# Attention in 64x64 quarters of the array: 21 blocks of 64 keys of four heads a batch instead of 24 blocks of 112 keys of two heads

## The chip, the cores and the metric

The kernel runs on one core of a Trainium2 chip. The time is device microseconds (us) of one execution. Three runs of the kernel before gave 609.70, 611.04 and 614.22 us: a median of 611.04. TensorE (PE in the profile, its weight loads PEld) multiplies matrices out of SBUF into the eight PSUM banks, ScalarE (ACT) and VectorE (DVE) read those banks, GpSimd (POOL) and SyncE (SP) mainly start DMA transfers; POOL also does some arithmetic on SBUF.

## The reference

`q`, `k` and `v` are float32 [8 batches, 12 heads, 448 tokens, 64]. Per batch and head the reference computes

```
scores = (q @ k.T) / 8
attn   = max(scores, 0)**2 / 448          # no softmax, so blocks of keys simply add up
x[b, :, head*64:(head+1)*64] = attn @ v
```

and then, per batch, on x [448, 768]:

```
u   = x + real(fft(fft(x, over tokens), over channels))
un  = (u - mean(u)) / sqrt(var(u) + 1e-6)             # per token
out = u + max(un @ w_ch1, 0) @ w_ch2                  # 768 -> 3072 -> 768
```

All 8 x 448 tokens go through the two large products (the FFN below).

## The kernel before

**Order of the work.** The kernel is one long unrolled program. Its order is found while it is built by a planner, `Streams.run` (lines 79 to 111). Each stage is a generator that yields `need(engine, duration, deps, buffers, ok)`. The planner keeps a time for each engine, takes the stage that could start earliest (ties by a rank), moves that engine's time by the duration and lets the generator issue its instructions. So the durations written in the code (`mm`, `act`, `dve`, `SWITCH = 0.13`, 0.85 for a load) only decide the order; the chip runs each engine's instructions in that order and waits where data are late. The stages are `loading` (POOL), `turning` (transposes of q and k), `attention(b)`, `mix(b)` with `mix_rows` (both transforms, the sum u, its normalisation), `ffns`, and `warming`, which puts idle matmuls (line 1135) wherever PE has nothing else before the first batch is through. `attention(b)` may run ahead of the FFN by up to `LEAD = 1.9` batches: `progress` counts finished FFN work in batches.

**PSUM.** `BS` is three pairs of banks (tiles `psS`, [128, 2, 512]) and `BF` two single banks (tiles `psF`). Scores, the transforms and `mix_rows` use BS; the FFN, the values and the transposes of q and k on PE use BF.

**Loads** (`load_group`, line 303). A batch has three groups of four heads. For each group and each of q, k, v there is one DMA from POOL, which also turns float32 into bf16. The tile has R = 112 partitions with 4 heads x 4 neighbouring tokens x 64 numbers: runs of 1 KB read, 512 bytes written.

**Turning q and k.** For batches 0 and 1 on PE (`turn_on_pe`, line 424: 16 transposes of 112x64 for each half of a group, both q and k in one BF bank, then one copy to SBUF, line 429, on DVE or ACT). For later batches DVE reorders the tile (`qkr`, line 392) and SP starts a DMA transpose into `qkT` (line 401).

**Attention** (`attention`, from line 485). A *block* is 112 keys (every fourth token) of a pair of heads against all 448 queries; a batch has `NB = 4 * MC` = 24.
- Scores, line 540: two matmuls of 64 contraction rows by 112 columns, one head in each half of the array's rows, 448 queries streamed, into the two banks of a BS pair.
- `squares`: ACT takes the relu of both heads from PSUM (line 561, 112 x 896), DVE squares it (line 567). `NSQ` = 9 such tiles.
- Values, line 525: for one pair of heads, four blocks, each two matmuls of 112 contraction rows by 64 columns, one head in each half of the array's columns, added up in one BF bank.
- `fold` (lines 448 to 471): DVE takes that bank out with two scaled copies (`xT`, tokens back in order, the second half reversed), adds and subtracts the two halves (lines 459, 460), and in the second half of a batch combines the two of them (`diff`, lines 469, 471). `turn_x` (line 480) starts a DMA transpose of `xT` from SP.

One step of `attention` is a *burst* on PE: if four squared blocks wait, their values, then up to three blocks of scores, then back to the FFN. For batch 0 (`few`) scores come singly and before values. When six values are done, `mix(b)` follows: line 954 (line 929 for batch 0), 970, then `mix_rows` 794 to 846, stores to DRAM and DMA transposes back (`turn_un`, line 892), and `ffn(b)` with its products in lines 1085 and 1113.

**SP and POOL** take their DMA issues in the planner's order, each waiting for its data at the head of its queue.

Of the kernel before, what the change touches and what calls it, by code (L numbers as in the profile page):

```python
# [10 lines left out]
BF16 = mybir.dt.bfloat16  # L11
# [126 lines left out]
def kernel(  # L138
# [20 lines left out]
    HG = 4  # L159
    NG = H // HG  # L160
# [123 lines left out]
    GRP = 4 * R * HG * Dh * 4  # L284
# [4 lines left out]
    def load_group(i, which=(0, 1, 2)):  # L289

        b, g = divmod(i, NG)
        hs = slice(g * HG, (g + 1) * HG)
        for x, (nm, src) in enumerate((("q", q), ("k", k), ("v", v))):
            if x not in which:
                continue
            if b == 0 and x < 2:
                e = yield need("POOL", 0.85)
                t = first_qk[x][:R, g]
            else:
                e = yield need("POOL", 0.85, bufs=[BQ[x]])  # L300
                t = work.tile([R, HG, 4 * Dh], BF16, name=f"{nm}n", tag=f"{nm}n",
                              bufs=3 if nm == "v" else QN)
            nc.gpsimd.dma_start(out=t, in_=src[b, hs].rearrange("h (p j) d -> p h (j d)", j=4))  # L303
            loads[i][x] = t.rearrange("p h (j d) -> p j h d", j=4)

            ready[i][x].t = sch.dma(e, GRP, 360e3, "sw") + (1.5 if g else 0.0, 3.0, 14.0, 7.0)[min(b, 3)]
            if i == 0 and x == 1:
                yield need("POOL", 0.7)
                make_identity(nc, ident)
            if i == 0 and x == 2:  # L310
                e = yield need("POOL", 1.1)
                dft_indices()
                indices_ready.t = e + LATENCY["POOL"]
            if i == 2 and x == 2:
                yield need("POOL", 0.75)
                pads()
            if i == NG + 1 and x == 1:
                yield need("POOL", 1.8)
                mirrors()


    first_qk = [work.tile([128, NG, HG, 4 * Dh], BF16, name="qk0", tag="unT", bufs=2) for _ in range(2)]
# [42 lines left out]
    NSQ = 9  # L365
# [14 lines left out]
    def turning():  # L380

        for b in range(B):
            for g in range(NG):
# [5 lines left out]
                for x in range(2):  # L389
                    e = yield need("DVE", 0.42, [ready[b * NG + g][x]], [BQR] if x == 0 else [])  # L390
                    o = work.tile([R, 4, HG, Dh], BF16, name="qkr", tag=f"qkr{x}", bufs=QR)
                    nc.vector.tensor_copy(o, loads[b * NG + g][x])
                    BQ[x].free.append(e)
                    qk.append(o.rearrange("p c h d -> p (c h d)"))
                ts = []
                for x in range(2):
                    e = yield need("SP", 0.8, [e + LATENCY["DVE"]], [BQT] if x == 0 else [])
                    if x == 0:
                        both = work.tile([128, 2, 8, R], BF16, name="qkT", tag="qkT", bufs=2)
                    t = both[:, x]  # L400
                    nc.sync.dma_start_transpose(out=t, in_=qk[x])
                    ts.append(t.rearrange("q (c r) p -> q r c p", r=2))
                    e = sch.dma(e + 0.5, R * 2048, 180e3)
# [5 lines left out]
    def turn_on_pe(b, g):  # L409
# [3 lines left out]
        both = work.tile([128, 2, 8, R], BF16, name="qkT", tag="qkT", bufs=2)  # L413
        turned[b][g] = [both[:, x].rearrange("q (c r) p -> q r c p", r=2) for x in range(2)]
        for r in range(2):
            for x in range(2):
                e1 = yield need("PE", 4 * 0.07, ready[i][x:x + 1], [] if x else [BF],
                                lambda: b != 1 or tail[0] == 2 or tail[0] == 0 and g == 0)
                if x == 0:
                    ptf = BF.take()  # L420
                    pt = ptf.bitcast(BF16)
                for c in range(4):
                    for h in range(2):
                        nc.tensor.transpose(pt[h * Dh:(h + 1) * Dh, x * S + c * R:x * S + (c + 1) * R],  # L424
                                            loads[i][x][:, c, 2 * r + h, :], ident[:R, :R])

            en, copy = (("DVE", nc.vector.tensor_copy), ("ACT", nc.scalar.copy))[r if b > 0 or g == 0 else 0]
            e2 = yield need(en, 0.75 if en == "DVE" else act(2 * S), [e1 + LATENCY["PE"]])
            copy(both.rearrange("q x (c r) p -> q r x c p", r=2)[:, r],
                 pt[:, 0:2 * S].rearrange("q (x c p) -> q x c p", x=2, c=4))  # L430
            BF.give(ptf, e2)
            turned_at[b][g][r].t = e2 + LATENCY["ACT"]
# [9 lines left out]
    def fold(b, m, F, av, av_end):  # L442
        e1 = yield need("DVE", 2 * dve(HS) + 2 * dve2(NS), [av_end],
                        [BX[m]] + ([BA[m]] if m < 3 else []))
        x = xTc[m]

        at = av[:, 0:S].rearrange("q (j p) -> q p j", j=4)
        nc.vector.tensor_scalar(x[:, 0:HS].rearrange("q (p j) -> q p j", j=4), at[:, 0:R // 2],  # L448
                                1.0 / (64.0 * S), None, op0=ALU.mult)
        xb, ab = x[:, XH + 1:XH + NS].rearrange("q (p j) -> q p j", j=4), at[:, R - 1:R // 2 - 1:-1, ::-1]  # L450
        nc.vector.tensor_scalar(xb, ab, 1.0 / (64.0 * S), None, op0=ALU.mult)  # L451
        BF.give(av, e1 - 2 * dve2(NS))
        if b > 0:
            sch.add(turn_x(b, m, e1 - 2 * dve2(NS) + LATENCY["DVE"]), (1, 1))
        else:
            x_ready[b][m].t = e1 + LATENCY["DVE"]
# [28 lines left out]
    def attention(b):  # L485


        F, sqs, fresh = [], {}, []
        NB = 4 * MC
        p = pa = 0  # L490
        while pa < NB:
            few = b == 0 or progress[0] == 0.0
            n = min(1 if few else 3, NB - p)
            ma = pa // 4

            lag = 3 if few else 2 if b < 3 else 1
            old = fresh[-lag] if len(fresh) >= lag else 0
            values = pa + 4 <= old if n else True
            n = max(0, min(n, NSQ - (p - pa - 4 * values)))
            values = values or not n  # L500
            fresh.append(p + n)
            deps, bufs, dur = [], [], 0.0
            if values:
                deps += [sqs[i][1] for i in range(pa, pa + 4)]
                bufs.append(BF)
                if b == 1:
                    deps.append(first_mixed)
                deps.append(ready[b * NG + ma // 2][2])
                dur += 4 * mm(S) + SWITCH
            if n:  # L510
                deps += [turned_at[b][i // 8][i // 4 % 2] for i in (p, p + n - 1)]
                bufs += [BS] * n
                dur += n * mm(S) + SWITCH
            lead = b + (p if n else pa) / NB - LEAD
            e = yield need("PE", dur + SWITCH, deps, bufs, lambda: progress[0] >= lead and (b != 1 or tail[0] == 2))
            av_end, scs = None, []

            for part in ("scores", "values") if few else ("values", "scores"):
                if part == "values" and values:
                    av = BF.take()  # L520
                    vn, h0 = loads[b * NG + ma // 2][2], 2 * ma % HG
                    for c in range(4):
                        sq = sqs.pop(pa + c)[0]
                        for h in range(2):
                            nc.tensor.matmul(av[h * Dh:(h + 1) * Dh, 0:S], lhsT=vn[:, c, h0 + h, :],  # L525
                                             rhs=sq[:, h, :], start=(c == 0), stop=(c == 3))
                        BSQ.free.append(e)
                    av_end = e - (n * mm(S) + SWITCH if n and not few else 0.0) + LATENCY["PE"]
                    if ma % 2 == 1:
                        BQ[2].free.append(e)  # L530
                    pa += 4
                if part == "values":
                    continue
                for i in range(p, p + n):
                    m, c = divmod(i, 4)
                    qT, kT = turned[b][m // 2]
                    sc = BS.take()
                    for h in range(2):
                        ps = slice(h * Dh, (h + 1) * Dh)
                        nc.tensor.matmul(sc[:R, h, 0:S].rearrange("k (c q) -> k c q", c=4),  # L540
                                         lhsT=kT[ps, m % 2, c, :], rhs=qT[ps, m % 2],
                                         start=True, stop=True)
                    scs.append((i, sc, e - SWITCH - (4 * mm(S) + SWITCH if values and few else 0.0)
                                - (p + n - 1 - i) * mm(S)))
                    if c == 3 and m % 2 == 1:
                        BQT.free.append(e)
                    if b == 0 and i == NB - 1:
                        first_scores.t = e
# [5 lines left out]
            if av_end is not None:  # L554
                yield from fold(b, ma, F, av, av_end)

    def squares(scs, sqs):
        for i, sc, t in scs:
            e = yield need("ACT", act(2 * S) - 0.03, [t + LATENCY["PE"]], [BSQ])
            r = sqs[i][0] = work.tile([R, 2, S], BF16, name="sq", tag="sq", bufs=NSQ)  # L560
            nc.scalar.activation(r, sc[:R, :, 0:S], AF.Relu)  # L561
# [578 lines left out]
    with tc.manual_schedule():  # L1140
# [8 lines left out]
        sch.add(attention(0), (0, 0))  # L1149
# [35 lines left out]
```

## Time and profile before

| | |
|---|---|
| median of three runs | 611.04 us |
| the profiled execution: its own time | 611.72 us |
| its span (first to last instruction) | 609.9 us |
| granted TensorE clock, mean | 0.997 of full speed |
| PE busy / weight loads | 596.6 us (98%) / 350.6 us (57%) |
| DVE busy | 338.6 us (56%) |
| ACT busy | 295.3 us (48%) |
| POOL busy | 156.7 us (26%) |
| DMA packets | 125,283, of them 40,304 on POOL's queue |
| FFN matmuls, lines 1085 and 1113 | 231.0 and 225.4 us busy |
| scores, line 540 / values, line 525 | 384 matmuls, 52.1 us / 384 matmuls, 45.5 us busy |

Busy time of PE counts the modelled length of each matmul, which overlaps the next one: 98% says that PE is rarely without work, not that it works at its peak. What matmuls cost is read from the distance between their starts. The page also has the chain that ended last: it goes back from the last instruction to what released it, and so on to the beginning; its shares say which lines set the end.

The time falls into parts that do not have the same limit: up to 9.4 us the first loads, to 39.5 us the attention of batch 0, to 59 us its transforms, from then on the FFN with the attention of later batches between its matmuls, and after 503.5 us the FFN alone.

### The profile page before, as it was taken

To read this page: it belongs to the slowest core of one execution; us is meant where nothing else is said; L and a number is where in the kernel's file an instruction comes from. 1 tells how busy PE (TensorE), PEld (TensorE's weight loads), DVE (VectorE), ACT (ScalarE), POOL (GpSimd) and SP (SyncE) were. 2 spreads that over 40 slices of the span, in tenths; PEclk is the share of its full clock that TensorE was granted. 3 is DMA by queue.
4 is the path that set the end of the run, shared out by engine and by line. 5 is a ranking of instruction groups with operands and counts; after the bars stand their busy time and mean duration, and the time that the engine had idled before them with its cause. 6 is when DMAs were issued, how large, how long until landed. Compare 5 with 4: busy or idle time off the path is not lost.

```text
span 609.9 us, 10759 instructions
## 1 busy us (share of the span) xinstructions
PE 596.6 (98%) x4314; PEld 350.6 (57%) x4314; DVE 338.6 (56%) x766; ACT 295.3 (48%) x448; POOL 156.7 (26%) x201
## 2 busy tenths in 40 slices
PE   8998999999999899999999999999999999999997
PEld 6567766577665465555445565555445565654464
DVE  6975776945688659555734468655743447110011
ACT  5965762387534567436653247535762245014300
POOL 8433031401246118211720127110620007000000
PEclk9998999999999999999999999999999999999999
DMA  9999999727978995977584675975461215420022
GB/s 128 207 209 228 209 171 156 177 68 103 136 154 179 191 183 164 178 134 120 172 152 104 121 125 190 150 153 98 144 136 60 87 51 174 115 93 14 1 81 76
DMA packets 125283, 82.22 MB, mean 135 GB/s; under 512 B 76352, under 2 KB 113248, under 8 KB 125232
## 3 DMA queue, kind: packets, MB, share of 16 engines
q0 software_dynamic: 40304, 34.02, 35.0%
q1 hardware_dynamic: 84928, 47.50, 33.8%
q8 instruction: 34, 0.56, 0.4%
q14 instruction: 17, 0.14, 0.1%
HBM read 62.91 MB, written 26.64 MB: 147 GB/s over the span
## 4 chain that ended last, share of the span: by engine, by line
PE 82%; DMA 6%; DVE 5%; issue 2%; POOL 2%; ACT 1%; SPq 1%; DVEq 0%; POOLq 0%; ACTq 0%
PE psF L1085 34%; PE psF L1113 32%; PE psF L525 6%; PE psS L540 6%; PE psS L954 2%; DMA w<-in_moe_w_ch_dram 2%; PE psS L794 1%; DMA qn<-in_q_dram 1%; DVE stats L826 1%; DMA vn<-in_v_dram 1%; DMA unT<-nbot 1%; DMA ntop<-un 1%; DVE u L815 1%; POOL qk L303 1%; DVE sq L567 1%
## 5 line engine op out<-in xcount | busy, mean ns | idle before, releaser
L1085 PE MATMUL psF<-unT,w 128*128 128x256 bf16 (+3 forms) x1440 | 231.0, 317 | 3.2 <-DMA unT<-nbot 2.0
L1113 PE MATMUL psF<-w,hT 128*128 128x384 bf16 (+2 forms) x1344 | 225.4, 326 | 0.0
L561 ACT ACTIVATE sq<-psS 112x896 bf16<-112x896 f32 x192 | 164.8, 917 | 119.6 <-PE psS L540 119.4
L1085 PEld LDWEIGHTS <-w 128*128 128x128 bf16 x1440 | 133.3, 99 | 94.3 <-issue 16.4
L1113 PEld LDWEIGHTS <-hT 128*128 128x128 bf16 x1344 | 129.0, 98 | 93.2 <-issue 10.2
L1047 ACT ACTIVATE hT<-psF 128x512 bf16<-128x512 f32 (+1 forms) x177 | 98.0, 555 | 108.8 <-PE psF L1085 107.6
L567 DVE TENSOR_TENSOR sq<-sq 112x896 bf16<-112x896 bf16 x192 | 119.3, 639 | 44.6 <-ACT sq L561 43.4
L1056 DVE TENSOR_TENSOR o<-psF,o 128x384 f32<-128x384 f32 (+2 forms) x56 | 31.0, 554 | 108.7 <-PE psF L1113 108.0
L303 POOL DMA_DIRECT2D vn<-in_v_dram x24 | 17.3, 721 | 177.3 <-PE psF L525 159.7
L448 DVE TENSOR_SCALAR xT<-psF 128x224 bf16<-128x224 f32 x48 | 18.8, 391 | 66.6 <-PE psF L525 66.6
L540 PE MATMUL psS<-qkT 64*112 64x448 bf16 x384 | 52.1, 366 | 2.3 <-ACT unT L780 1.5
L814 POOL TENSOR_TENSOR u<-tp,xn 128x385 f32<-128x385 f32 (+1 forms) x14 | 16.3, 1167 | 116.6 <-DVE tp L805 104.8
L525 PE MATMUL psF<-sq,vn 112*64 112x448 bf16 x384 | 45.5, 359 | 0.0
L540 PEld LDWEIGHTS <-qkT 64*112 64x112 bf16 x384 | 20.5, 125 | 26.4 <-issue 20.6
L525 PEld LDWEIGHTS <-vn 112*64 112x64 bf16 x384 | 17.6, 109 | 21.3 <-issue 13.6
L843 POOL TENSOR_SCALAR un<-u,rstd,nmr 128x768 bf16<-128x768 f32 (+1 forms) x24 | 28.0, 1170 | 6.2 <-DVE nmr L835 5.9
L826 DVE BATCH_NORM_STATS2 stats<-u 128x6 f32<-128x384 f32 (+1 forms) x56 | 28.1, 538 | 0.0
L303 POOL DMA_DIRECT2D qn<-in_q_dram x21 | 15.4, 734 | 13.9 <-PE psF L424 8.6
L1135 PE MATMUL psS<-warm 128*128 128x126 bf16 (+1 forms) x206 | 17.7, 239 | 1.3 <-DVE warm L216 1.3
L451 DVE TENSOR_SCALAR xT<-psF 128x224 bf16<-128x224 f32 x48 | 18.5, 386 | 0.0
L1135 PEld LDWEIGHTS <-warm 128*128 128x128 bf16 x206 | 13.5, 108 | 6.3 <-issue 4.6
L303 POOL DMA_DIRECT2D kn<-in_k_dram x21 | 15.3, 728 | 2.6 <-DVE diff L469 1.5
(120 smaller groups left out, 366.9 us busy)
## 6 DMA issues: line engine op xcount, KB each, us to landing
out_dram<-o SPq DMA_DIRECT2D x24, 384.0 KB, 2.3
vn<-in_v_dram POOLq DMA_DIRECT2D x24, 224.0 KB, 5.1
qn<-in_q_dram POOLq DMA_DIRECT2D x21, 224.0 KB, 6.4
kn<-in_k_dram POOLq DMA_DIRECT2D x21, 224.0 KB, 7.3
w<-in_moe_w_ch_dram POOLq DMA_DIRECT2D x12, 384.0 KB, 13.7
w<-in_moe_w_ch_dram POOLq DMA_DIRECT2D x4, 1152.0 KB, 22.2
utop<-u SPq DMA_DIRECT2D x8, 384.0 KB, 2.4
o<-utop SPq DMA_DIRECT2D x7, 384.0 KB, 4.7
```

The lines of the kernel that those rows point to most:

```text
L303: nc.gpsimd.dma_start(out=t, in_=src[b, hs].rearrange("h (p j) d -> p h (j d)", j=4))
L525: nc.tensor.matmul(av[h * Dh:(h + 1) * Dh, 0:S], lhsT=vn[:, c, h0 + h, :], rhs=sq[:, h, :], start=(c == 0), stop=(c == 3))
L540: nc.tensor.matmul(sc[:R, h, 0:S].rearrange("k (c q) -> k c q", c=4), lhsT=kT[ps, m % 2, c, :], rhs=qT[ps, m % 2], start=True, stop=True)
L561: nc.scalar.activation(r, sc[:R, :, 0:S], AF.Relu)
L567: nc.vector.tensor_tensor(r, r, r, op=ALU.mult)
L826: nc.vector.bn_stats(stats[:n, hf, :], u[:n, hf * (D // 2):(hf + 1) * (D // 2)])
L843: nc.gpsimd.tensor_scalar(un[:n], u[:n], rstd[:n, i:i + 1], nmr[:n, i:i + 1], op0=ALU.mult, op1=ALU.add)
L1047: nc.scalar.activation(h, p, AF.Relu)
L1056: nc.vector.tensor_tensor(o[:, hs], pc[:, 0:w], o[:, hs], op=ALU.add)
L1085: nc.tensor.matmul(ph[:, i * w:(i + 1) * w], lhsT=w1_sb[m][hf][:, jj * 128:(jj + 1) * 128], rhs=unT[:, m, c0:c0 + w], start=(m == 0), stop ...
L1113: nc.tensor.matmul(pc[:, 0:w], lhsT=hT[j // 4][:, j % 4, c * 128:(c + 1) * 128], rhs=w2_sb[j // 6][:, j % 6, hs], start=(j == 0), stop=(j ...
L1135: nc.tensor.matmul(first_pps[0][:, t, c0:512], lhsT=warm[:, 0:128], rhs=warm[:, c0:512], start=not begun, stop=False)
```

## The change

Every group of four heads is now laid out on all 128 partitions: partition (m, p) holds head pair m of the group and seven neighbouring tokens (J = 7 = 448/64). A block becomes 64 keys of all four heads, 7 blocks a group, 21 a batch.

- Loads: two DMAs for each of q, k, v, one for the even and one for the odd heads, with runs of 7 x 64 numbers.
- Scores: four matmuls of 64 rows by 64 columns. Values: four of 64 rows by 64 columns; the two row halves write different banks, so a group's values (seven blocks, four heads) take a pair of banks. For batches from 1 on that is a BS pair instead of a BF bank; for batch 0 it is both BF banks.
- Squares: 21 tiles of 128 x 896 a batch instead of 24 of 112 x 896; NSQ is 10.
- Turning: on PE, 14 transposes of 128x64 each for q and for k, each in a BF bank with its own copy; by DMA, a 128 x 896 source instead of 112 x 1024.
- `fold` handles a group: two head pairs, their four scaled copies, then the additions (`fold_one`). Six folds a batch as before, but two of them become ready together.
- A burst has seven blocks of values and up to two of scores, or up to three of scores alone. Batch 0 has its own `first_attention` and `first_values`; in its last group the values are given in two parts, six blocks and one.

The core of the diff:

```diff
+    J = S // 64
...
-                t = work.tile([R, HG, 4 * Dh], BF16, name=f"{nm}n", tag=f"{nm}n",
+                t = work.tile([128, 2, J * Dh], BF16, name=f"{nm}n", tag=f"{nm}n",
                               bufs=3 if nm == "v" else QN)
-            nc.gpsimd.dma_start(out=t, in_=src[b, hs].rearrange("h (p j) d -> p h (j d)", j=4))
-            loads[i][x] = t.rearrange("p h (j d) -> p j h d", j=4)
+            for h in range(2):
+                if h:
+                    e = yield need("POOL", 0.72)
+                nc.gpsimd.dma_start(out=t[:, h], in_=src[b, hs].rearrange("(m h) (p j) d -> h m p (j d)", h=2, j=J)[h])
+            loads[i][x] = t.rearrange("p h (j d) -> p j h d", j=J)
...
-    NSQ = 9
+    NSQ = 10
...
-                    o = work.tile([R, 4, HG, Dh], BF16, name="qkr", tag=f"qkr{x}", bufs=QR)
+                    o = work.tile([128, J, 2, Dh], BF16, name="qkr", tag=f"qkr{x}", bufs=QR)
...
+        for x in range(2):
+            e1 = yield need("PE", 2 * J * 0.04, ready[i][x:x + 1], [BF],
+                            lambda: b != 1 or tail[0] == 2 or tail[0] == 0 and g == 0)
+            ptf = BF.take()
+            pt = ptf.bitcast(BF16)[:, 0:J * 128].rearrange("q (j p) -> q j p", j=J)
+            for j in range(J):
+                for h in range(2):
+                    nc.tensor.transpose(pt[h * Dh:(h + 1) * Dh, j, :], loads[i][x][:, j, h, :], ident)
+
+            en, copy = (("DVE", nc.vector.tensor_copy), ("ACT", nc.scalar.copy))[x if b > 0 or g == 0 else 0]
...
+    def fold(b, g, F, avs, av_end, give):
+        for h in range(2):
+            m = 2 * g + h
+            e1 = yield need("DVE", 2 * dve(HS), [av_end], [BX[m]])
...
+            give(h, e1)
+            if b > 0:
+                sch.add(turn_x(b, m, e1 + LATENCY["DVE"]), (1, 1))
+            else:
+                x_ready[b][m].t = e1 + LATENCY["DVE"]
+                yield from fold_one(b, m, F)
+        if b > 0:
+            for h in range(2):
+                yield from fold_one(b, 2 * g + h, F)
...
-        NB = 4 * MC
+        NB = NG * J
         p = pa = 0
         while pa < NB:
+            few = progress[0] == 0.0
+            g = pa // J
+            values = pa + J <= p - 2 or p == NB
+            n = min(1 if few else 2 if values else 3, NB - p, NSQ - (p - pa - J * values))
             deps, bufs, dur = [], [], 0.0
             if values:
+                deps += [sqs[i][1] for i in range(pa, pa + J)] + [ready[b * NG + g][2]]
                 if b == 1:
                     deps.append(first_mixed)
+                bufs.append(BS)
+                dur += J * mm(S) + SWITCH
             if n:
+                deps += [c for i in (p, p + n - 1) for c in turned_at[b][i // J]]
                 bufs += [BS] * n
+                dur += n * mm(S)
             lead = b + (p if n else pa) / NB - LEAD
             e = yield need("PE", dur + SWITCH, deps, bufs, lambda: progress[0] >= lead and (b != 1 or tail[0] == 2))
+            if values:
+                held = BS.take()
+                avs = [held[:, m] for m in range(2)]
+                weigh(b, g, avs, sqs, range(J))
...
+            if values:
+                yield from fold(b, g, F, avs, e - n * mm(S) + LATENCY["PE"], lambda m, t: BS.give(held, t) if m else None)
+
+    def score(b, i, e):
+        g, j = divmod(i, J)
+        qT, kT = turned[b][g]
+        sc = BS.take()
+        for h in range(2):
+            ps = slice(h * Dh, (h + 1) * Dh)
+            for m in range(2):
+                ks = slice(m * 64, (m + 1) * 64)
+                nc.tensor.matmul(sc[ks, h, 0:S].rearrange("k (j p) -> k j p", j=J),
+                                 lhsT=kT[ps, j, ks], rhs=qT[ps, :, ks], start=True, stop=True)
...
+    def weigh(b, g, avs, sqs, js):
+        vn = loads[b * NG + g][2]
+        for j in js:
+            sq = sqs[g * J + j][0]
+            for m in range(2):
+                ks = slice(m * 64, (m + 1) * 64)
+                for h in range(2):
+                    nc.tensor.matmul(avs[m][h * Dh:(h + 1) * Dh, 0:S], lhsT=vn[ks, j, h, :],
+                                     rhs=sq[ks, h, :], start=(j == 0), stop=(j == J - 1))
+
+    def first_attention():
+
+        F, sqs = [], {}
+        for i in range(NG * J):
+            e = yield need("PE", mm(S), turned_at[0][i // J], [BS])
+            sqs[i] = [None, Cell()]
+            sch.add(squares([(i, score(0, i, e), e)], sqs), (0.2, 0.2))
+            if i % J == J - 1:
+                sch.add(first_values(i // J, F, sqs), (0.1, 0.1))
+        first_scores.t = e
+
+    def first_values(g, F, sqs):
+        held = None
+        for js in ((0, J),) if g < NG - 1 else ((0, J - 1), (J - 1, J)):
+            e = yield need("PE", (js[1] - js[0]) * mm(S),
+                           [sqs[g * J + j][1] for j in range(*js)] + [ready[g][2]], [BF, BF] if js[0] == 0 else [])
+            if held is None:
+                held = [BF.take(), BF.take()]
+            weigh(0, g, held, sqs, range(*js))
+            BSQ.free += [e] * (js[1] - js[0])
+        BQ[2].free.append(e)
+        yield from fold(0, g, F, held, e + LATENCY["PE"], lambda m, t: BF.give(held[m], t))
...
-            r = sqs[i][0] = work.tile([R, 2, S], BF16, name="sq", tag="sq", bufs=NSQ)
-            nc.scalar.activation(r, sc[:R, :, 0:S], AF.Relu)
+            r = sqs[i][0] = work.tile([128, 2, S], BF16, name="sq", tag="sq", bufs=NSQ)
+            nc.scalar.activation(r, sc[:, :, 0:S], AF.Relu)
...
-        sch.add(attention(0), (0, 0))
+        sch.add(first_attention(), (0, 0))
```

## The prediction

> **What bounds the kernel now.** First the page's busy table, the chain and the groups.
>
> ```profile
> PE 596.6 (98%) x4314; PEld 350.6 (57%) x4314; DVE 338.6 (56%) x766; ACT 295.3 (48%) x448; POOL 156.7 (26%) x201
> ...
> PE 82%; DMA 6%; DVE 5%; issue 2%; POOL 2%; ACT 1%; SPq 1%; DVEq 0%; POOLq 0%; ACTq 0%
> ...
> L561 ACT ACTIVATE sq<-psS 112x896 bf16<-112x896 f32 x192 | 164.8, 917 | 119.6 <-PE psS L540 119.4
> ...
> L303 POOL DMA_DIRECT2D qn<-in_q_dram x21 | 15.4, 734 | 13.9 <-PE psF L424 8.6
> ```
>
> PE is the bound: 82% of the chain is PE work, and ACT's relu of the scores waits 119.4 us for PE, not the reverse. Then the waits of PE itself over the whole span:
>
> ```profile
> PE psF L1085 <- DMA unT<-nbot: 2.0, 1, 2.0
> PE psF L424 <- DVE qkT L429: 1.9, 1, 1.9
> PE psS L540 <- ACT unT L780: 1.5, 1, 1.5
> ```
>
> There are three real stalls, and all lie where a batch's FFN begins: at 51 us (batch 0, second part), 119 us (batch 1) and 208 us (batch 2). There a chain of DVE, ACT, SP and DMA steps is later than PE. From 210 us PE never waits again for more than 0.9 us. So a nanosecond of PE work is worth a nanosecond after 210 us, and maybe less before.
>
> Then the timeline of PE in a quiet stretch, where starts are what counts:
>
> ```profile
> 299.69 2.54 PE L1085 MATMUL psF<-unT,w 128*128 128x512 bf16 x11
> 302.16 0.95 PE L525 MATMUL psF<-sq,vn 112*64 112x448 bf16 x8
> 303.03 0.78 PE L540 MATMUL psS<-qkT 64*112 64x448 bf16 x6
> 303.74 2.55 PE L1085 MATMUL psF<-unT,w 128*128 128x512 bf16 x11
> ```
>
> Values start at 302.16, scores at 303.03, FFN at 303.74: four pairs in 0.87 us, three pairs in 0.71. Inside a burst the starts of single matmuls show the two of a pair 3 ns apart and pairs 189 ns apart: 448 columns at full rate, two matmuls at once. What is left over is the change of shape: the last pair of values is followed after 0.283 us instead of 0.189, and the first pair of scores takes 0.045 more than the others. So a stretch of scores costs 0.71 - 3 x 0.189 = 0.143 us beyond its pairs, one of values 0.87 - 0.756 = 0.12.
>
> **PE work, batches 1 to 7.** I summed the stretches of lines 525 and 540 in PE's timeline, from the first start of a stretch to the next instruction of another line:
>
> | from, us | values matmuls | scores matmuls | bursts | time, us |
> |---|---|---|---|---|
> | 59 to 119.4 | 48 | 54 | 10 | 11.4 |
> | 119.4 to 210.2 | 80 | 84 | 16 | 20.4 |
> | 210.2 to the end | 208 | 198 | 38 | 46.2 |
>
> Together 78.0 us for 336 pairs (63.5 us) and 98 stretches (14.5 us). After the change there are 7 x 42 = 294 groups of four matmuls. Going through the loop of `attention` with 21 blocks gives nine bursts a batch (three with values), as many as now, but scores and values have one shape, so a burst is one stretch: 63 x 0.143 = 9.0 us. What four matmuls on quarters cost no row shows. Lower end: 189 ns, all four at once. Upper end: 378 ns, two pairs in turn. I take 189, because both halves of it stand in the rows: scores run concurrently in two row halves, values in two column halves, each at 189 ns. Issue doesn't forbid it: the transposes of line 424 (eight q and eight k matmuls in 0.45 us from 68.63 to 69.08, each with its own weights) start every 25 ns, so four start in 100 ns. Sum: 294 x 0.189 + 9.0 = 64.6 us, against 78.0: **-13.4 us**, by the same working about -7.2 of it after 210 us and -6.2 before.
>
> **Weight loads** are four for each block instead of two, each half as wide for scores. In the values burst above the rows are:
>
> ```profile
> 302.15 0.52 PEld L525 LDWEIGHTS <-vn 112*64 112x64 bf16 x8 [0.42 <-issue]
> ```
>
> All eight loads are over by 302.67, before the last pair of matmuls starts at 302.75: they lie under matmuls in the same rows of the array. A rule of the Trainium skill speaks against the change here: "TensorE: Matmul & The Clock Gate", Part 3 (packing small matmuls), says that a weight load overlaps running matmuls only when it is for other rows of the array, and column neighbours share their rows. By that rule the present values would show it too, and this row disagrees. What the rule would give is rival 2.
>
> **Batch 0, to 39.5 us.** PE isn't the bound: line 1135's idle matmuls fill its gaps. From 9.4 to 36.0 us ACT is: its 24 relus take 20.2 us of that stretch, 0.84 each, and DVE is nearly as full. Three relus fewer: -2.5 us. Against it: the last fold covers two head pairs one after another, which puts another two copies and two additions (0.71 + 0.46 us by the spacing in rows 448 to 460) behind the last values, while the last values are one block, not four (-0.57): +0.6. The loads: 26 issues instead of 13 on POOL, whose queue also holds the identity matrix and the indices from which DVE and ACT build the transforms' tables.
>
> ```profile
> 8.64 0.70 POOL L303 DMA_DIRECT2D vn<-in_v_dram  x1
> ...
> 17.70 0.53 POOL L332 DMA_DIRECT2D w<-in_moe_w_ch_dram  x1 [0.33 <-DMA vn<-in_v_dram]
> ```
>
> A load of 448 runs costs 0.70 us to issue, a weight load of 128 rows 0.53. The new ones have 128 runs of 1.8 KB, so they are nearest to 0.53; the bounds are 0.53 and 0.70, a pair costing 0.36 to 0.70 us more than one now. Over the six loads of q and k up to the third group, and the v loads between, that is 3 to 5 us at the last issue, but today the DMA engines, not POOL, set the pace: 448 packets of 512 bytes take 1.15 us at the rate from 15 to 20 us (about 390 packets a microsecond), and for the last of these loads, issued at 8.64, POOL still waits at 17.70. The new 256 packets of 896 bytes, between 60 ns (512 bytes) and 134 ns (1,536 bytes) a packet about 88 ns, take 0.97 us. So the later issue is mostly hidden by that queue: 0 to +2.6 us, I take +1.3. Sum for batch 0: -0.6 us. If the tables come later than the relus, the 1.3 grows, and that is in the range.
>
> **From 59 to 210 us** the -6.2 us is not all kept. The stalls at 119 and 208 us end chains from the last values of a batch through fold, the transforms, normalisation and transposes. PE that is faster only waits longer there, unless the last values come earlier too. The last fold now has two head pairs: 1.4 us of copies, 0.9 of additions, 1.6 of combining, against 2.05 in the rows from 97.08 to 99.13: about +2 us on the chain to line 954. For the other side, the last values of batch 1 should come some 2 us earlier (nine bursts at today's spacing). I keep half: -3.1 us.
>
> **Nothing for:** ACT and DVE after 59 us (three relus and squares fewer a batch, but off the path: ACT is under 50% and DVE under 60% busy from 210 us); the DMA transposes of q and k (same bytes) and their DVE copies; the PE transposes of batches 0 and 1 (28 of 128 columns for 32 of 112); POOL's extra 0.36 us a load later on, since POOL idles 103.3 us for values there. Values holding a BS pair take it from scores for seven blocks (1.3 us) and the fold's copies (1.4); a burst comes every 8 us or so against ACT's 2.5 us for three blocks, so the FFN covers it. If that cover is gone, bursts come later in the FFN, and PE still has FFN work until a batch's end.
>
> **Sum** against the profiled execution's 611.72 us (span 609.9 and 1.8 around it): -7.2 - 3.1 - 0.6 = -10.9, so 600.8. That execution is 0.7 us above the median of the runs; I forecast **600.5**.
>
> **Rivals.**
> 1. *The gain of the first 210 us is lost to the chains* and the first batches are late as well: -7.2, loads +2.6, two stalls 2 us longer: about 611. For it: all three stalls are there. Against: batch 0 has less ACT work. Chance 0.15.
> 2. *The weight load of a quarter is not hidden* (slower). Each block then pays 109 ns (line 525's mean load) on top of 189: 294 x 0.298 + 9 = 96.6 us of attention, +18.6: 630 us. The gain is gone from about 234 ns a block, (78.0 - 9.0) / 294. Against it: the row of loads above; for it: nothing here shows four shapes at once. It is what the rule of the Trainium skill named above would give. Chance 0.09.
> 3. *The quarters don't run four at once*, so that the change doesn't do what it says: 378 ns a block, 120 us, +42: 653 us. Chance 0.05.
> 4. *Batch 0's new order stalls* (both BF banks held by values while the next turning wants one): 4 us of held banks (seven blocks, four copies, an addition) in each of two groups, 8 us: 609. Chance 0.05.
>
> The forecast's own case, 593 to 606, has 0.66. The range 592 to 616 takes in rivals 1 and 4 and leaves out 2 and 3. A measurement of this kernel tells about 1% (6 us) from no change. Faster by over 1% (under 605): 0.65, the forecast's case without its last microsecond; within: 0.21, that and rivals 1 and 4; slower: 0.14, rivals 2 and 3.
>
> **What would show it.** Four matmuls of 64*64 some 3 ns apart and the next four 189 ns later; no 0.28 us between values and scores; nine bursts a batch, one of values each seven blocks. ACT's last relu of batch 0 at about 34 us instead of 36.0. Line 1085 first at 45 to 47 us. PE's stall at batch 2 two or three us longer. After 210 us the FFN reaching its end about 7 us sooner. The prediction is wrong if blocks start over 200 ns apart, or if a new stall of several microseconds stands before 120 us.

## The result, and the profile after

The changed kernel takes **738.62 us** (median of four runs, 736.77 to 743.42), the kernel before 611.63 (four runs beside it): a ratio of 1.2085, with an interval from 1.2009 to 1.2161. It is 21% slower where 2% faster was forecast, outside the range (592 to 616) and slower than any rival (653 at most). The profiled execution took 743.42 us, its span 741.6.

The lines of its page that answer to those shown before. In the new code scores are line 542, values 555, the relu 585, the FFN 1109 and 1137, the loads 307:

```profile
PE 623.0 (84%) x4988; PEld 366.2 (49%) x4988; DVE 330.5 (45%) x742; ACT 276.7 (37%) x424; POOL 214.7 (29%) x273
...
DMA packets 241640, 82.82 MB, mean 112 GB/s; under 512 B 206528, under 2 KB 229600, under 8 KB 241584
...
q0 software_dynamic: 156656, 34.54, 52.3%
...
PE 42%; DMA 10%; DVE 2%; POOL 1%; ACT 1%; issue 0%; SPq 0%; DVEq 0%; ACTq 0%
...
L307 POOL DMA_DIRECT2D vn<-in_v_dram x48 | 38.3, 803 | 191.0 <-PE psS L542 109.2
```

PE is down from 98% to 84% of the span. The chain's shares add up to only 56% here, because it can be followed back no further than 320 us; PE has 42 of those 56 points, where it had 82 of all 100 before. ACT and DVE have less to do and hardly a share of the chain. What has grown is DMA, from 6 points of 100 to 10 of 56, and the odd row is the number of packets: 156,656 on POOL's queue instead of 40,304, for nearly the same bytes. The section of the page on DMA issues says the same from the other end (size of one, median us from issue to landing); first the kernel before, then the changed one:

```profile
vn<-in_v_dram POOLq DMA_DIRECT2D x24, 224.0 KB, 5.1
qn<-in_q_dram POOLq DMA_DIRECT2D x21, 224.0 KB, 6.4
kn<-in_k_dram POOLq DMA_DIRECT2D x21, 224.0 KB, 7.3
```

```profile
vn<-in_v_dram POOLq DMA_DIRECT2D x48, 112.0 KB, 13.7
qn<-in_q_dram POOLq DMA_DIRECT2D x42, 112.0 KB, 17.9
kn<-in_k_dram POOLq DMA_DIRECT2D x42, 112.0 KB, 16.7
```

Half the bytes take two to three times as long. How that reaches PE can be read in the changed kernel's timeline, first DVE from 196 us, then PE in the same stretch (in brackets the idle time before an instruction and what ended it):

```profile
202.80 0.62 DVE L396 COPY qkr<-qn 128x896 bf16<-128x896 bf16 x1 [10.96 <-DMA qn<-in_q_dram]
203.34 0.38 DVE L448 TENSOR_SCALAR xT<-psS 128x224 bf16<-128x224 f32 x1
203.63 0.39 DVE L451 TENSOR_SCALAR xT<-psS 128x224 bf16<-128x224 f32 x1
207.63 0.62 DVE L396 COPY qkr<-kn 128x896 bf16<-128x896 bf16 x1 [3.61 <-DMA kn<-in_k_dram]
208.17 0.38 DVE L448 TENSOR_SCALAR xT<-psS 128x224 bf16<-128x224 f32 x1
208.47 0.39 DVE L451 TENSOR_SCALAR xT<-psS 128x224 bf16<-128x224 f32 x1
```

```profile
198.19 0.38 PE L542 MATMUL psS<-qkT 64*64 64x448 bf16 x4
208.91 0.59 PE L542 MATMUL psS<-qkT 64*64 64x448 bf16 x4 [10.34 <-DVE xT L451]
```

DVE waits 10.96 us for a load of q at the head of its queue. Behind it stand the copies that empty the values' pair of banks, half of them behind a second wait, for k. PE's next scores want that pair and wait 10.34 us; the FFN matmuls behind them in PE's order wait too. Over the whole run the wait of scores for these copies is the largest of PE:

```profile
PE psS L542 <- DVE xT L451: 33.2, 3, 13.4
PE psF L1109 <- DMA unT<-nbot: 15.4, 1, 15.4
PE psS L542 <- DMA qkT<-qkr: 10.3, 3, 5.3
```

There is a second price: around such pauses the granted clock falls to half. The changed kernel has sixteen stretches at half clock, the last moments included, 131 us together (mean clock 0.913), the kernel before one of 3.4 us and its last moments.

### The profile page after: what moved, and what is told of

It is laid out like the page before. It is cut to its first block, busy times and chain, and to the rows that moved or that the text cites. A ratio compares the mean times of both kernels' runs of the same rounds, so it can differ in the third digit from the quotient of the medians.

```text
span 741.6 us, 12129 instructions
## 1 busy us (share of the span) xinstructions
PE 623.0 (84%) x4988; PEld 366.2 (49%) x4988; DVE 330.5 (45%) x742; ACT 276.7 (37%) x424; POOL 214.7 (29%) x273
## 3 DMA queue, kind: packets, MB, share of 16 engines
q0 software_dynamic: 156656, 34.54, 52.3%
## 4 chain that ended last, share of the span: by engine, by line
PE 42%; DMA 10%; DVE 2%; POOL 1%; ACT 1%; issue 0%; SPq 0%; DVEq 0%; ACTq 0%
PE psF L1109 19%; PE psF L1137 17%; DMA kn<-in_k_dram 6%; DMA out_dram<-o 2%; DMA o<-ubot 2%; PE psS L555 2%; PE psS L542 2%; PE psS L818 1%; PE psS L978 1%; DVE sq L591 1%; POOL qn L307 0%; DVE u L838 0%; POOL vn L307 0%; DVE o L1080 0%; DVE stats L850 0%
## 5 line engine op out<-in xcount | busy, mean ns | idle before, releaser
L585 ACT ACTIVATE sq<-psS 128x896 bf16<-128x896 f32 x168 | 145.6, 917 | 186.3 <-PE psS L542 184.5
L591 DVE TENSOR_TENSOR sq<-sq 128x896 bf16<-128x896 bf16 x168 | 102.6, 629 | 50.8 <-ACT sq L585 50.7
L307 POOL DMA_DIRECT2D vn<-in_v_dram x48 | 38.3, 803 | 191.0 <-PE psS L542 109.2
L542 PE MATMUL psS<-qkT 64*64 64x448 bf16 x672 | 50.4, 380 | 45.2 <-DVE xT L451 33.2
L542 PEld LDWEIGHTS <-qkT 64*64 64x64 bf16 x672 | 16.8, 108 | 67.7 <-issue 49.4
L307 POOL DMA_DIRECT2D kn<-in_k_dram x42 | 33.8, 825 | 34.7 <-DMA qn<-in_q_dram 20.6
L307 POOL DMA_DIRECT2D qn<-in_q_dram x42 | 33.9, 823 | 18.2 <-DMA vn<-in_v_dram 15.5
L448 DVE TENSOR_SCALAR xT<-psS 128x224 bf16<-128x224 f32 x42 | 16.2, 385 | 48.1 <-PE psS L555 48.1
L555 PE MATMUL psS<-sq,vn 64*64 64x448 bf16 x588 | 33.0, 358 | 1.8 <-DVE sq L591 1.4
L555 PEld LDWEIGHTS <-vn 64*64 64x64 bf16 x672 | 18.2, 108 | 18.3 <-issue 9.1
```

The lines of the kernel that those rows point to most:

```text
L307: nc.gpsimd.dma_start(out=t[:, h], in_=src[b, hs].rearrange("(m h) (p j) d -> h m p (j d)", h=2, j=J)[h])
L542: nc.tensor.matmul(sc[ks, h, 0:S].rearrange("k (j p) -> k j p", j=J), lhsT=kT[ps, j, ks], rhs=qT[ps, :, ks], start=True, stop=True)
L555: nc.tensor.matmul(avs[m][h * Dh:(h + 1) * Dh, 0:S], lhsT=vn[ks, j, h, :], rhs=sq[ks, h, :], start=(j == 0), stop=(j == J - 1))
L585: nc.scalar.activation(r, sc[:, :, 0:S], AF.Relu)
L591: nc.vector.tensor_tensor(r, r, r, op=ALU.mult)
```

## The experiments

The question was first whether the loads explain the loss, and how; then what is left without them. "Before" is 611.6 to 612.0 us in all of these comparisons.

| run | us, median | ratio to before | FFN of batch 0, 1, 2 starts, us | packets of 4 bytes, POOL's queue |
|---|---|---|---|---|
| before | 611.6 | 1 | 46.6, 121.9, 210.2 | 1,856 |
| the change | 738.6 | 1.209 | 61.3, 159.9, 294.2 | 132,032 |
| e1 loads cut by head pair | 616.0 | 1.006 (1.003 to 1.009) | 50.8, 126.3, 221.4 | 3,008 |
| e2 before, two engines | 715.2 | 1.168 (1.161 to 1.174) | | 115,904 |
| e3 before, four engines | 643.7 | 1.051 (1.045 to 1.057) | | 51,392 |
| e4 only v on two engines | 675.2 | 1.103 (1.094 to 1.111) | | 46,016 |
| e5 e1, three edits of the start | 624.4 | 1.019 (1.016 to 1.022) | 45.9, 127.1, 232.8 | |
| e6 e1, lead 2.0 | 615.8 | 1.005 (1.002 to 1.008) | 50.8, 124.9, 221.9 | |
| e7 e5 and e6 | 624.0 | 1.020 (1.016 to 1.025) | 45.9, 126.6, 230.2 | |
| e8 before, lead 2.0 | 611.2 | 1.001 (0.998 to 1.004) | | |
| e9 e1, two edits of the start | 611.7 | 1.000 (0.997 to 1.002) | 47.4, 125.2, 219.4 | |
| e10 e9, batch 2 turned on PE | 603.2 | 0.986 (0.982 to 0.990) | 47.5, 123.1, 204.2 | |
| e11 before, batch 2 turned on PE | 608.5 | 0.996 (0.994 to 0.998) | 46.6, 121.9, 207.5 | |
| e12 e1, batch 2 turned on PE | 609.8 | 0.994 (0.991 to 0.998) | 50.8, 125.0, 207.6 | |

### The loads: e1 to e4

The kernel before has 1,856 packets of 4 bytes on POOL's queue, which is 16 for each of its 116 DMAs. The changed kernel has 132,032. If its 44 DMAs that aren't loads of q, k or v have 16 each as before, its 144 loads have 912 each, and 912 is 14 x 64 + 16. The load is written as 2 x 64 x 448 numbers: a slowest dimension of 2. So the guess was that each load's 128 runs lie on two DMA engines, 64 each, and that the other fourteen get packets of 4 bytes as fillers. The trace doesn't name the engine of a packet, so this had to be tested by its consequences. The packets of the data fit: 18,432 of 896 bytes, median 88 ns, both as forecast, but from 3 to 6 us, under the first loads, only 3.7 of them were under way at a time on average, against 18.7 of 512 bytes before.

e1 cuts the same load the other way:

```diff
-                nc.gpsimd.dma_start(out=t[:, h], in_=src[b, hs].rearrange("(m h) (p j) d -> h m p (j d)", h=2, j=J)[h])
+                nc.gpsimd.dma_start(out=t[h * 64:(h + 1) * 64],
+                                    in_=src[b, g * HG + 2 * h:g * HG + 2 * h + 2].rearrange("h (p j) d -> p h (j d)", j=J))
```

> The changed kernel with one edit: its two loads for each of q, k and v are cut by head pair (64 partitions, two heads) instead of by even and odd heads (128 partitions, one head of each pair). The same bytes go to the same places, so the output is the reference's; only the order of the dimensions of the DMA differs: 64 x 2 x 448 numbers instead of 2 x 64 x 448. Theory A (two engines): the loads of the changed kernel run on two DMA engines each, because their slowest dimension has the size 2, and that alone makes it slow. Sign of it in the changed kernel: 912 packets of 4 bytes for each load DMA, which is 14 idle engines x 64 plus the 16 at the end, where the kernel before has 16. Then this kernel has 16 a DMA (about 3,000 in all), and its time is the blind forecast's: 600.5 us, 594 to 610. Rival B (order): the new order of batch 0 and the values' hold on a pair of banks make it slow and the loads only follow; then 690 us or more. Rival C (number of issues): twice as many DMA issues on POOL cost the time; then also 690 or more, as there are as many here.

e2 puts loads like the changed kernel's into the kernel before, e3 the same with four:

```diff
-            nc.gpsimd.dma_start(out=t, in_=src[b, hs].rearrange("h (p j) d -> p h (j d)", j=4))
+            for s in range(2):
+                nc.gpsimd.dma_start(out=t[:, 2 * s:2 * s + 2].rearrange("p h c -> p (h c)"),
+                                    in_=src[b, hs].rearrange("(m h) (p j) d -> h m p (j d)", h=2, j=8)[s])            # e2
+                                    in_=src[b, hs, s * 224:(s + 1) * 224].rearrange("m (p j) d -> m p (j d)", j=8))  # e3
```

> The kernel before with its loads alone changed: two DMAs for each of q, k and v, each with the even or the odd heads of a group, read as 2 x 56 x 512 numbers into 112 partitions. The bytes and the tiles are the same, but the tokens land elsewhere, so the output is not the reference's; the work is the same. Theory A: slowest dimension 2, so two engines a DMA: 14 x 56 + 16 = 800 packets of 4 bytes for each load DMA, some 116,000 in all, and a time near the changed kernel's: 690 to 760 us. Rival B: the loads are not the cause, 612 us +- 8. Rival C: the number of issues is as in the changed kernel, 690 or more.

> As the run before, but the two DMAs of a load take half of the tokens each of all four heads: 4 x 28 x 512 numbers. Again bytes, tiles and work are the same and the output is not the reference's. Theory A: four engines a DMA, 12 x 28 + 16 = 352 packets of 4 bytes for each load DMA, some 51,000 in all; loads take about half as long as on two engines, so the time lies clearly between: 620 to 680 us. Rival B: 612 +- 8. Rival C (number of issues alone): the same time as the run before.

e4 is e1 for q and k and the changed kernel for v.

> The changed kernel with q and k loaded by head pair as in the first run and v left by even and odd heads. The output is the reference's. Theory A: a third of the loads stay on two engines: some 46,000 packets of 4 bytes (48 x 912 + 96 x 16 + 700). The values are needed later than the scores, so most of the loss goes: 605 to 660 us. Rival B: 690 or more.

The counts came out as worked out beforehand, to the packet for e1 (16 a DMA), e2 (800) and e3 (352). The data packets under way from 3 to 6 us go with them: 2.8 in e2, 7.4 in e3, 16.4 in e1. The times: one rearranged load takes 738.6 to 616.0 us, and in the kernel before, whose arithmetic is untouched, two engines a load cost 103 us and four 32. The number of issues is the same in e1, e2 and e3, so rival C falls; the order of the new code is the same in e1 and in the change, so rival B falls for all but the last few microseconds. e4 was slower than expected (675, not 605 to 660). Its q and k go over all engines by their counts, but land late as well:

```profile
vn<-in_v_dram POOLq DMA_DIRECT2D x48, 112.0 KB, 12.6
qn<-in_q_dram POOLq DMA_DIRECT2D x42, 112.0 KB, 12.6
kn<-in_k_dram POOLq DMA_DIRECT2D x42, 112.0 KB, 11.7
```

They are late where a load of v is ahead of them: a load of q issued at 134.6 us, when the last v has landed, takes 4.7 us, and one at 155.6 us, 0.8 us behind a load of v, takes 15.8. In e1 the three rows are 4.4, 5.7 and 5.8 us: sooner than before, with half the bytes in each.

A rule of the Trainium skill says this outright. "DMA: Bandwidth & Descriptors", section "Why a DMA increments its semaphore by 16 and not by 1", states that the number of engines is the largest one up to 16 that divides the slowest dimension of both sides, and its "Rules for kernel authors" warn of an outermost dimension smaller than 16. The counts of e1, e2 and e3 agree with it for 16, 2 and 4. It was not weighed in the prediction.

### What is left: e5 to e8

e1 was still 4 us over the kernel before where the forecast was 11 under. In e1's trace two places are late. The FFN of batch 0 starts at 50.8 us, not 46.6. And batch 2's FFN waits 7.0 us instead of 2.0, as PE's waits in e1 show:

```profile
PE psF L1110 <- DMA unT<-nbot: 7.0, 1, 7.0
PE psS L543 <- DVE unT L805: 2.1, 1, 2.1
PE psF L426 <- DVE qkT L430: 1.9, 1, 1.9
```

During that wait, at 216.1 us, the granted clock falls to half, for 10.2 us, about half of them after the FFN has begun at 221.4.

e5 changes three places of the start:

```diff
-            en, copy = (("DVE", nc.vector.tensor_copy), ("ACT", nc.scalar.copy))[x if b > 0 or g == 0 else 0]
+            en, copy = (("DVE", nc.vector.tensor_copy), ("ACT", nc.scalar.copy))[x if b > 0 else 0]
...
                 make_identity(nc, ident)
-            if i == 0 and x == 2:
                 e = yield need("POOL", 1.1)
                 dft_indices()
...
-                            lambda: b != 1 or tail[0] == 2 or tail[0] == 0 and g == 0)
+                            lambda: b != 1 or tail[0] == 2)
```

> The changed kernel with its loads cut by head pair (the first run, e1, 616.0 us) and three edits of the order in the first 60 us, nothing else: the indices from which the transforms' tables are built come before the first load of v on POOL; for batch 0 both copies of the turned q and k are on DVE, where the first group's k was on ACT behind three sine tables; batch 1 is not turned before batch 0 is through, so that it holds no single bank when the last values of batch 0 want both. Theory: batch 0 of e1 is late because of these three places. There the first score stands at 11.68 us (8.90 in the kernel before), the last values at 39.63 us behind the copy that frees a single bank at 39.8, and the FFN starts at 50.76 us (46.63). With the edits: indices 1.3 us earlier, the copy on ACT gone (0.9 us), the wait for banks gone (1.7 us): FFN from 46.5 to 47.5 us and the time 612 us (610 to 614). Rival: the later issue of the halved loads sets batch 0's pace; then the FFN starts at 49.5 us or later and the time stays at 616 +- 1.5.

e6 and e8 set `LEAD = 2.0` in e1 and in the kernel before; e7 is e5 with it.

> e1 with one number changed: attention may run 2.0 batches ahead of the FFN instead of 1.9. Theory: e1's wait of 7.0 us at the start of batch 2's FFN (2.0 in the kernel before) comes from batch 2's chain starting too late, and its idle time then drops the granted clock to half for 10.2 us from 216 us on, which costs another 2.5 us once the FFN has started. Starting the attention a tenth of a batch (some 8 us) earlier takes the chain's end below the FFN's start: wait under 2 us, no half clock there, and 616.0 - 5 - 2.5 = 608.5 us (606 to 611). Rival: the chain is bound by its DMA transposes among the loads, which then also come earlier and collide again; wait of 5 us or more and 614 to 618 us.

> Both edits of the two runs before. If the two losses are separate they add up: 616.0 - 4 - 7.5 = 604.5 us (601 to 608), near the blind forecast of 600.5 and faster than the kernel before (611.9). If one is only moved into the other, 610 or more.

> The kernel before with 2.0 instead of 1.9 batches of lead, as a control: what the earlier attention is worth without the quarters. Theory: the kernel before waits 2.0 us at batch 2's FFN and keeps its clock there, so at most that goes: 610 us (608.5 to 612). Rival: its lead was set right for it and other transfers collide: 613 or more.

The start came even sooner than expected in e5 (first score at 8.8 us, FFN at 45.9), but the total was 624 us, not 612. PE's waits show the new ones:

```profile
PE psF L1137 <- DMA w<-in_moe_w_ch_dram: 8.1, 2, 6.3
PE psF L1109 <- DMA unT<-nbot: 7.5, 1, 7.5
PE psS L542 <- DMA qkT<-qkr: 6.1, 2, 4.1
```

The weights that PE waits for are `w_ch2`. POOL issues nothing between 34.2 and 52.2 us in e5, where its next instruction, the normalisation of batch 0 in line 716, waits 18.1 us for its data; the next loads of q, k and v come after it, and the first part of `w_ch2` at 64.9 us (51.0 in e9 below, which lacks only the third edit). So the third edit is the cause. That it works through the planner, which places loads later when the turning frees their buffers later, is read from the code and not shown. e6's theory was wrong too: with more lead the last values of batch 2 start at the same 166.4 us as in e1 and its transforms at 174.5, so the lead doesn't bind batch 2, and 7.4 us of wait stayed. e7 has e5's loss again. e8 shows no difference.

### A version faster than both: e9 to e12

e9 drops e5's third edit. e10 adds another way for batch 2: its normalised rows are turned by PE into the FFN's tile, as batch 1's are, and don't go through DRAM and DMA transposes. e11 and e12 are that edit alone, in the kernel before and in e1. The core of it:

```diff
+            if b == 2:
+                nr, idn, to = ((128, ident, ((0, 0, 128),)), (128, rev[:, 0:63], ((321, 0, 63),)),
+                               (96, ident[:96, :96], ((128, 0, 96),)),
+                               (97, rev[:97, 31:128], ((224, 0, 97),)))[2 * ch + i]
+                sch.add(turn_rows(un, e + 0.2, nr, idn, to, ("DVE", "ACT")[i], third_un[2 * ch + i], 2), (1, 1))
...
+        elif b == 2:
+            yield need("SP", 0.0, third_un + n_stored[2][1:2])
```

> e1 (616.0 us) with two of the three edits of e5: the indices before the first load of v, and both copies of batch 0's turned q and k on DVE. Batch 1 is turned where e1 turns it. Theory: e5's first 46 us were as meant (FFN at 45.9 us instead of 50.8), and its loss came from the third edit alone: the loads of batch 1 wait on POOL for q and k's buffers, and the second half of the weights is queued behind them (8.1 us of waits for weights). Without that edit no wait of PE for weights, the FFN starts at 47.5 to 49 us and the time is 613.5 us (612 to 615). Rival: the first two edits alone move the weights too: 618 or more.

> e9 with batch 2 brought to its FFN as batch 1 is: its normalised rows are turned by PE (24 matmuls, four copies) instead of being stored to DRAM and turned by two DMA transposes; only the 64 rows that belong to the next group still go through DRAM. Theory: e1's wait of 7.0 us before batch 2's FFN is made of that store (7 us to landing) and that transpose (10.5 us), so the wait goes, the half clock of 10.2 us after it goes (2.5 us lost after the FFN's start), and PE pays 4 x 0.33 us for the matmuls: 613.5 - 7.0 - 2.5 + 1.3 = 605.5 us (603 to 609), faster than the kernel before (611.7). Rival: the chain is late before the store (fold of two head pairs, normalisation on POOL); then over 3 us of the wait stay and the time is 609 or more.

> The kernel before with the same edit for batch 2, as a control. Its wait there is 2.0 us and its clock stays full, so the edit is worth at most 2.0 - 1.3: 611 us (610 to 612.5). If it is worth several microseconds here too, what the run before wins is not the quarters' but the edit's.

> e1 with the edit for batch 2 alone, without the two edits of the start. Theory: the two losses are separate, so this gives 616.0 - 7.0 - 2.5 + 1.3 = 608 us (606 to 611). Rival as for e10: 612 or more.

e9 takes 611.7 us, 4.3 less than e1, with the FFN at 47.4 us and no wait for weights. e10 takes 603.2 us and is faster than the kernel before by 1.4% (1.0 to 1.8). Its page and its longest waits of PE:

```profile
PE 586.5 (98%) x4966; PEld 351.8 (59%) x4980; DVE 332.8 (55%) x745; ACT 276.3 (46%) x425; POOL 188.2 (31%) x272
...
PE 85%; DMA 6%; DVE 4%; POOL 3%; ACT 1%; issue 1%; SPq 0%; DVEq 0%; POOLq 0%; ACTq 0%
```

```profile
PE psF L425 <- DVE qkT L429: 2.2, 1, 2.2
PE psS L542 <- DVE unT L805: 1.4, 1, 1.4
```

The wait before batch 2's FFN and the half clock after it are gone. The edit is worth 8.5 us on top of e9 and 6.2 on top of e1. In the kernel before it is worth 3.1 to 3.5 us (e11), more than the 0.7 that was expected there at most. So part of e10's gain is the edit's own, and the larger part repairs what the quarters had made worse. Between e11 and e10, which both have it, lie 5.4 us; e10 also has the two edits of the start, and still its first FFN begins 0.9 us later than e11's.

## Why the prediction was wrong

**PE work: right.** Here is a burst of e1 (scores are line 543, values 556, FFN 1110), to compare with the one of the prediction:

```profile
154.77 0.93 PE L1110 MATMUL psF<-unT,w 128*128 128x256 bf16 x7
155.63 1.52 PE L556 MATMUL psS<-sq,vn 64*64 64x448 bf16 x28
156.98 0.55 PE L543 MATMUL psS<-qkT 64*64 64x448 bf16 x8
157.46 0.72 PE L1110 MATMUL psF<-unT,w 128*128 128x256 bf16 x5
```

The four matmuls of a block start 3 to 4 ns apart (155.629 to 155.639). The second block follows the first after 214 ns, and from there on blocks follow after 189 ns (156.032, 156.221, 156.410 and so on); scores follow the last values after 189 ns too (156.789 to 156.978). Seven blocks take 1.35 us with the change of shape before them, two of scores 0.48 with the one after. So rivals 2 and 3, weight loads in the open or pairs in turn, are refuted, and the rule of the Trainium skill that the prediction sets against the change doesn't hold for this form. Attention's stretches of batches 1 to 7 sum to 66.3 us in e10, some 63 without two stalls in it, where 64.6 was worked out. The 78.0 of before also holds a stall, of 1.5 us at 119 us, so about 13 us of PE work were saved, as forecast. In the changed kernel the same sum is 120.5 us, because its stretches hold the waits.

**Loads: the step that failed.** "The new 256 packets of 896 bytes, between 60 ns (512 bytes) and 134 ns (1,536 bytes) a packet about 88 ns, take 0.97 us. So the later issue is mostly hidden by that queue." The packets are there, with that size and that time. But the 0.97 us takes over the rate of the kernel before (about 390 packets a microsecond), as if the new loads were spread over the engines like the old ones, and by all counts above they ran on two. The step looked at the size of the runs and at POOL's time to issue, not at how the dimensions are ordered. It was priced at 0 to +2.6 us and was worth +122.6 (738.6 to 616.0). For the same reason it was wrong to put nothing for "POOL's extra 0.36 us a load later on": issuing one of the confined loads takes 0.80 to 0.83 us, and what matters is that it lands 9 to 12 us later than a load of the kernel before. In e1 the issue takes 0.62 to 0.64 us, between the bounds of 0.53 and 0.70.

**Batch 0:** forecast -0.6 us up to the FFN. Measured in e1: +4.1. The relus were fewer, but three places were late, as e5 showed by removing them (45.9 us, -0.8). With two of them removed (e9) ACT's last relu ends at 34.0 us, as forecast. Two are what the prediction named: the tables behind POOL's longer issue (DVE begins them at 5.85 us instead of 4.42), and rival 4's mechanism, values waiting for both single banks (39.63 us, after the copy for batch 1 at 38.86; the edit that ends this wait is worth 1.5 us, 47.4 in e9 and 45.9 in e5). The third it missed: the first group's k was copied by ACT behind three sine tables.

**59 to 210 us:** "I keep half" of 6.2. That was -3.1 us. In e1 none of it was kept: from the first FFN to batch 2's it takes 170.6 us and the kernel before 163.6, which is +7.0. The wait for batch 2 became 7.0 us, not "two or three us longer" than 2.0, and the clock fell during it. The direction of the wait was named, its size and the clock were not. The chains show where the size comes from. The DMA transpose that ends the wait, first in the kernel before, then in e1, is issued 6.8 us later and also takes 4.4 us more:

```profile
204.09 6.02 DMA unT<-nbot
```

```profile
210.90 10.45 DMA unT<-nbot
```

The step counted some 2 us for the longer fold and left the transpose as it was. Why it takes longer in e1 is not shown; without it (e10) the wait is gone.

**After 210 us:** forecast -7.2. From the start of batch 2's FFN to the end, e1 takes 391.3 us and the kernel before 399.6; e1's count includes about half of the stretch at half clock, and more of its attention lies before that point. From the next FFN on (e1 282.4, before 274.1) it is 330.3 against 335.7 us: 5.4 less.

**The rivals** had no case in which the loads themselves become slow, so 738.6 lay outside all of them. The last step of the sum is also uneven: 600.8 less 0.7 is 600.1, not 600.5. And that e10's 603.2 us lies near the forecast doesn't bear the forecast out: e1, which is the changed kernel with its loads on all engines, takes 616.0, and e10 has three more edits that the forecast knew nothing of.

## What to carry to other kernels

A DMA's cost has three readings, not two: bytes a run, issue time, and over how many engines its slowest dimension spreads it. The number of packets on the page gave it away at once (156,656 for 40,304); when a load's dimensions are reordered, work out the spread for its source and its destination before anything else. And a gain on the bound engine is kept only if the chains that end at its few waits are looked at one by one: here a saving of 13 us in PE work was worth nothing until the start and one transpose had been put in order.

## What the runs showed of the hardware

- With k engines and n runs on each, (16 - k) x n + 16 gives the packets of 4 bytes for each load on POOL's queue in all four kernels: 912, 800, 352 and 16 in the change, e2, e3 and e1. Most of them take 7 to 9 ns each; in the changed kernel they take 184 us of 16 engines' time together. The few engines for the data and the fillers come from the same cut of the load, and no run separates what each of them costs.
- Apart from the last moments of a run, the half clock came in stretches that are multiples of 3.41 us (3.41, 6.83, 10.24, 17.07). e1's stretch began at 216.1 us, 1.7 us into a wait of PE, and ended 4.9 us after its matmuls were back.
- DVE's copy that reorders q and k before the DMA transposes (line 392 before, 396 after) takes a median of 0.61 to 0.62 us for 128 x 896 numbers, where it took 0.42 for 112 x 1024. Why, and what it costs, stays open.
